# Softmax remainders and PSUM evictions moved between engines in a chain of three attention and feed-forward layers

## Chip, core and metric

The kernel runs on one core of a Trainium2 chip. The metric is the device time of one execution in microseconds (us); the median of three runs stands for a kernel.

## What is computed

Three layers in float32, each feeding the next, cut here to what matters:

```python
# 1: attention, B=4, H=8, S=1152, D=64; queries are pooled by two: T=576
q_pool = q.reshape(B, H, S // 2, 2, D).mean(axis=3)
a = softmax(q_pool @ k.T / sqrt(D));  x = a @ v            # x: (B, T, H*D = 512)
# 2: four causal attention heads over x, each token weighted by its two best gates
for e in range(4): out += gate[e] * (softmax(causal((x @ wq[e]) @ (x @ wk[e]).T / 8)) @ (x @ wv[e])) @ wo[e]
# 3: token shift, k = relu(xk @ w_k), r = sigmoid(xr @ w_r), result r * ((k * k) @ w_v)
```

## The kernel before

Layer 1 works head by head, 32 heads (four batches of eight). A head has nine **steps**; a step makes two score tiles of 128 keys by 288 queries in one PSUM buffer `st` (two such buffers), with two rounded (float32r) matmuls each (L760, L761: rounded keys and queries, then the products of their remainders and the row of the maxima). ScalarE takes the exponential into `p` (L768). The weighted sums over the keys follow four steps later (`LAG`), in one of two forms, which a table of nine entries per head chooses:

- **native** (`'n'`): one full-precision matmul a tile, `p` with the values `VF` (L788);
- **split**: `p` is copied into a rounded `ph` by the engine of the entry's first letter (L64 is ScalarE, `'s'`), the remainder `pl = p - ph` is taken by that of the second (L71; `'g'` is POOL, `'v'` is VectorE), and three rounded matmuls a tile follow: L795 and L796 (`ph` with rounded values and their remainders, in `VV`) and L797 (`pl`).

Ahead of a head the maxima of its scores are found: fifteen matmuls of 384 keys (L730), each reduced by VectorE from one of four PSUM banks (L732); L403 and L408 finish them. The weighted sums themselves occupy banks of the same four. When a sum is complete, `copy_eps` reads its bank into `U` (L142 on VectorE, L140 on ScalarE), and after a division (L254, and L256 with the gate) and a broadcast through DRAM (`R`), L817 writes the head's part of `XT`. `s2_split` turns a batch's `XT` into a rounded `XH` (L269) and a remainder `XL` (L270); `s1_vsplit` does so with the values of a head (L610, L611). `copy` is the helper behind L64 (ScalarE), L66 (VectorE) and L68 (POOL), `lo_of` that behind L71.

From batch 1 on, the steps of layer 2 for the batch before are set between the steps of layer 1 (`s2_job`: L470 to L476 scores, L482 exponentials, L498 sums, L531 the product with the gate). Weights of layer 3 are split into rounded parts in chunks `w3st` (L887 to L920). Layer 3 itself runs at the end (L1101, L1124, L1137).

The order of work comes from `drive`, which runs the steps one by one and lets each task (maxima, transposes, loads, splits) run its parts between two given steps, and from a scheduler that then places every instruction in its engine's queue.

The table that the change edits is `G` (L26); it is read where the work is built:

```python
how = G["SA" if hh == 0 else "SB" if hh == 1 else "S1" if b else "S0"][si]
copy(how[0], ph, pt)                                   # L774, in the step
lo_of(how[1], pl, pt, ph)                              # L780, two steps later
copy_eps(G["ua" if hh < 2 else "u1" if b else "u0"], U[...], acc[j][: D + 1, :HT])
copy_eps(G["u2"], U[...], acc[j][: D + 1, :HT])        # L523, layer 2
copy(G["vvh"] if hh > 2 else G["ve"], vt[:, :, 0:D], vr)
copy(G["xh"], XH[:, p], XT[:, p])
```

Of the kernel before, what the change touches and what calls it, by code (L numbers as in the profile page):

```python
# [22 lines left out]

P = 128
D = 64
G = {'LAG': 4, 'LO': 2, 'nf1': 2, 'nfx': 1, 'mxA': (0, 5), 'prA': (0.5, 5.0), 'mx0': (-2.0, 7.0), 'mx1': (-2.5, 6.0), 'vl': (0.0, 1.5), 'vs': (5.5, 1.0), 'pr0': (0.5, 5.0), 'pr1': (0.5, 4.0), 'ld': (6.5, 5.5), 'm2': (2.0, 1.5), 'nm': 0, 'nm2': 0, 'dup': 2, 'mid': 1, 'bc': 1, 'end': 9, 'mid2': 2, 'end2': 4, 'spl': 9, 'gate': 8, 'gate2': 2, 'w2': (2, 30), 'w3': (7, 14), 'S0': ('n', 'sv', 'sg', 'n', 'sv', 'n', 'sv', 'sv', 'sv'), 'S1': ('sg', 'sg', 'sv', 'sg', 'sg', 'sg', 'sv', 'n', 'sg'), 've': 'g', 'kh0': 's', 'kh1': 'v', 'qh0': 's', 'qh1': 's', 'kq': 's', 'kl': 'v', 'rs': 'v', 'rl': 'v', 'ym': 'g', 'yo': 'v', 'LGe': 'v', 'p1': (5, 5, 5, 9), 'p2': (9, 9, 9), 'p3': (2,), 'p4': (9, 9, 9, 9), 'p5': (8, 8, 8, 8), 'p6': (9, 9, 9), 'po': (2, 4, 5, 9), 'add0': 'g', 'add1': 'g', 'xt': 'v', 'u1': 'v', 'u2': 'v', 'y2': 'v', 'yh': 's', 'yl': 'v', 'xo': 'v', 'v2': 's', 'xh': 'g', 'xl': 'v', 'vvh': 'g', 'vvl': 'g', 'klo': 'v', 'HB': 3, 'PB': 6, 'blk': 1, 'm2w': 2, 'order': 2, 'kdup': 0, 'L2': 4, 'O2': 1, 'a0': (5.0, 5.0), 'a1': (2.0, 2.5), 'a2': (0.0, 1.0), 'a3': (2.0, 2.0), 'r0': 2, 'NV': 2, 'NF': 2, 'SA': ('n', 'vg', 'sg', 'n', 'sv', 'n', 'sv', 'sv', 'sv'), 'SB': ('n', 'sv', 'sv', 'n', 'vv', 'n', 'sv', 'sv', 'sv'), 'ua': 'v', 'u0': 'v', 'xt0': 'v', 'w3d': 8, 'w3q': (3, 27), 'WC': 1, 'kb': 1, 'kst': 1, 'qst': 0, 'CW': 512, 'wt': 'v', 'wl': 'v', 'wa': 'v', 'WB': 1, 'mxg': 2, 'hq': 's', 'hpos': (0, 1, 11, 20)}  # L26
NEG = -1.0e30

TINY = 1.17e-9
# [26 lines left out]
def tile_kernel(ctx: ExitStack, tc: tile.TileContext, q, k, v, w_gate, wq, wk, wv, wo,  # L56
                mu_k, mu_r, w_k, w_v, w_r, out):
    nc = tc.nc
    LAG, LO, HB = G["LAG"], G["LO"], G["HB"]
    eng = {"g": nc.gpsimd, "v": nc.vector, "s": nc.scalar}  # L60

    def copy(e, dst, src):
        if e == "s":
            nc.scalar.activation(dst, src, AF.Copy)  # L64
        elif e == "v":
            nc.vector.tensor_copy(dst, src)  # L66
        else:
            nc.gpsimd.tensor_scalar(dst, src, 1.0, 0.0, op0=ALU.mult, op1=ALU.add)  # L68

    def lo_of(e, dst, src, hi):  # L70
        eng[e].tensor_tensor(dst, src, hi.bitcast(F32), op=ALU.subtract)  # L71
# [88 lines left out]
    def later(n, fn):  # L160
        pending.append((now[0] + n, fn))
# [82 lines left out]
    def normaliser(U, gate, name):  # L244
# [8 lines left out]
        def mid():  # L253
# [3 lines left out]
            nc.sync.dma_start(scr.rearrange("o (p i) -> (o p) i", p=D), rd)  # L257
            later(G["bc"], bcast)

# [43 lines left out]
    def s2_gate(b):  # L303
# [3 lines left out]
        def f():  # L307
# [22 lines left out]
            def g():  # L330
# [973 lines left out]
```

## Time and profile before

| | before |
|---|---|
| median of 3 runs | 1107.34 us (1106.95 to 1110.87) |
| profiled execution | 1109.79 us |
| its span, first to last instruction | 1108.0 us |
| granted TensorE clock, mean | 0.987 |
| TensorE matmul busy | 1031.3 us, 93% |
| VectorE busy | 843.1 us, 76% |
| ScalarE busy | 550.4 us, 50% |
| POOL busy | 414.4 us, 37% |

Engines are named PE (TensorE matmul), PEld (its weight load), DVE (VectorE), ACT (ScalarE), POOL (GpSimd) and SP (SyncE, which issues the DMAs). An instruction's row names its line, engine, operation, what it writes and reads, and its shape. A busy share is an average over stages. A wait is put down to what ended it last by the profile. A full-precision matmul (L788) leaves two records, so a native step has four.

### The profile page before, as it was taken

The page shows a single profiled execution, that of the slowest core. Times are in us where ns is not written, and L with a number is a line of the kernel's source. Part 1 is how long each engine was busy: PE and PEld are TensorE (multiplying, and loading weights), DVE is VectorE, ACT ScalarE, POOL GpSimd, SP SyncE. Part 2 cuts the span into 40 slices and gives each one's busy share as a digit, 9 for nine tenths or more (in the row PEclk, how much of TensorE's full clock was granted, in tenths as well). Part 3 has the DMA queues.
Part 4 walks back from the last instruction along what each step waited for, and adds up shares of the span by engine and source line. Part 5 has one row for each costly group of instructions (what it writes and reads, how often), then busy time and mean ns, then how long its engine had stood idle before and what let it go on. Part 6 is the DMA issues. An engine that isn't in the chain of part 4 may idle for free.

```text
span 1108.0 us, 18910 instructions
## 1 busy us (share of the span) xinstructions
PE 1031.3 (93%) x6800; PEld 908.1 (82%) x6800; DVE 843.1 (76%) x1664; ACT 550.4 (50%) x922; POOL 414.4 (37%) x378
## 2 busy tenths in 40 slices
PE   5999998999999999999999999997997899999998
PEld 4788888888888887788888888886875788888887
DVE  5899998789999888989987877885777624444442
ACT  5567665556566555665555565563444312222222
POOL 7343327446345544543664445363002001111110
PEclk9899999999999999999999999999998999999999
DMA  4656544445544544554444333246354321111100
GB/s 113 144 153 141 131 118 118 106 120 142 143 116 103 149 126 124 132 141 124 109 129 113 87 92 87 71 130 199 113 163 137 114 81 39 40 39 39 39 20 20
DMA packets 129099, 119.29 MB, mean 108 GB/s; under 512 B 63751, under 2 KB 91358, under 8 KB 129006
## 3 DMA queue, kind: packets, MB, share of 16 engines
q1 hardware_dynamic: 129006, 118.08, 40.3%
q8 instruction: 54, 0.88, 0.3%
q14 instruction: 39, 0.32, 0.1%
HBM read 63.24 MB, written 20.07 MB: 75 GB/s over the span
## 4 chain that ended last, share of the span: by engine, by line
PE 62%; DVE 21%; DMA 8%; ACT 4%; issue 3%; SPq 1%; POOL 1%; DVEq 0%; ACTq 0%; POOLq 0%
PE stw L1137 9%; PE sth L1101 7%; PE bank L730 6%; PE st L760 5%; DVE PM L732 5%; PE st L761 4%; PE str L1124 4%; DMA R<-scr 4%; PE bank L797 3%; PE bank L795 3%; PE bank L796 3%; PE bank L788 3%; PE stq L354 3%; PE bank L498 3%; DVE pl L71 2%
## 5 line engine op out<-in xcount | busy, mean ns | idle before, releaser
L71 POOL TENSOR_TENSOR pl<-p,ph 128x576 fp32r<-128x576 f32 x152 | 230.6, 1521 | 208.9 <-ACT ph L64 115.7
L732 DVE TENSOR_REDUCE PM<-bank 128x1 f32<-128x384 f32 (+1 forms) x480 | 251.6, 543 | 30.3 <-PE bank L730 27.7
L768 ACT ACTIVATE p<-st 128x576 f32<-128x576 f32 x288 | 186.0, 648 | 117.0 <-PE st L761 111.9
L64 ACT ACTIVATE ph<-p 128x576 fp32r<-128x576 f32 x238 | 162.8, 685 | 57.8 <-PE bank L796 48.7
L730 PE MATMUL bank<-KA,QA 128*128 128x384 f32 (+1 forms) x480 | 177.8, 383 | 13.7 <-DVE KB L151 4.4
L760 PE MATMUL st<-QA,KA 128*128 128x288 f32 x576 | 177.5, 319 | 3.9 <-DVE LG L299 1.7
L761 PE MATMUL st<-QB,KB 65*128 65x288 f32 x576 | 167.5, 305 | 0.0
L797 PE MATMUL bank<-pl,VV 128*65 128x288 f32 x480 | 142.4, 297 | 8.4 <-DVE pl L71 6.1
L795 PE MATMUL bank<-ph,VV 128*65 128x288 f32 x480 | 145.0, 302 | 2.0 <-DVE PM L732 0.8
L796 PE MATMUL bank<-ph,VV 128*64 128x288 f32 x480 | 141.6, 295 | 0.0
L760 PEld LDWEIGHTS st<-QA,KA 128*128 128x128 f32 x576 | 110.9, 193 | 12.5 <-ACT p L768 4.0
L761 PEld LDWEIGHTS st<-QB,KB 65*128 65x128 f32 x576 | 110.7, 193 | 2.5 <-issue 0.2
L730 PEld LDWEIGHTS bank<-KA,QA 128*128 128x128 f32 (+1 forms) x480 | 87.1, 185 | 28.8 <-DVE PM L732 9.5
L1040 POOL TENSOR_SCALAR yxr<-x,omr 128x256 f32<-128x256 f32 x36 | 25.7, 730 | 196.3 <-DVE xkl L151 133.4
L1101 PE MATMUL sth<-xkh,wk 128*128 128x256 f32 x512 | 91.3, 279 | 1.2 <-ACT relu L1108 1.2
L71 DVE TENSOR_TENSOR pl<-p,ph 128x576 fp32r<-128x576 f32 x88 | 79.4, 903 | 1.8 <-ACT ph L64 1.1
L1101 PEld LDWEIGHTS sth<-xkh,wk 128*128 128x128 f32 x512 | 78.7, 188 | 1.9 <-ACT relu L1108 1.4
L1108 ACT ACTIVATE relu<-sth 128x512 f32<-128x512 f32 x32 | 17.5, 597 | 121.1 <-PE sth L1101 120.3
L797 PEld LDWEIGHTS bank<-pl,VV 128*65 128x65 f32 x480 | 65.3, 136 | 11.2 <-DVE pl L71 7.2
L795 PEld LDWEIGHTS bank<-ph,VV 128*65 128x65 f32 x480 | 66.1, 138 | 6.6 <-DVE PM L732 2.3
L1101 PE MATMUL sth<-xkl,wk 128*128 128x256 f32 x256 | 71.4, 279 | 0.0
L796 PEld LDWEIGHTS bank<-ph,VV 128*64 128x64 f32 x480 | 65.3, 136 | 6.3 <-issue 0.2
(209 smaller groups left out, 2326.0 us busy)
## 6 DMA issues: line engine op xcount, KB each, us to landing
KA<-sk SPq DMA_DIRECT2D x60, 160.0 KB
qr<-in_q_dram SPq DMA_DIRECT2D x32, 288.0 KB
kr<-in_k_dram SPq DMA_DIRECT2D x32, 288.0 KB
VF<-in_v_dram SPq DMA_DIRECT2D x32, 288.0 KB
KA<-sk SPq DMA_DIRECT2D x60, 128.0 KB
R<-scr SPq DMA_DIRECT2D x48, 144.0 KB
w3h<-w3st SPq DMA_DIRECT2D x20, 256.0 KB
w3l<-w3st SPq DMA_DIRECT2D x20, 256.0 KB
```

Source lines behind the costliest of these rows:

```text
L64: nc.scalar.activation(dst, src, AF.Copy)
L71: eng[e].tensor_tensor(dst, src, hi.bitcast(F32), op=ALU.subtract)
L730: nc.tensor.matmul(ps[:n, : 3 * P], QA[i][:, t0 : t0 + n], KA[i][:, 3 * g * P : 3 * (g + 1) * P], start=True, stop=True)
L732: nc.vector.tensor_reduce(pm[:n, c, g : g + 1], ps[:n, : 3 * P], axis=AX.X, op=ALU.max)
L760: nc.tensor.matmul(st[:, n, :HT], KA[i][:, ks], QA[i][:, cs], start=True, stop=False)
L761: nc.tensor.matmul(st[:, n, :HT], KB[i][0 : D + 1, ks], QB[i][0 : D + 1, cs], start=False, stop=True)
L768: nc.scalar.activation(pt, st[:, :, :HT], AF.Exp, scale=1.0 / 16.0)
L795: nc.tensor.matmul(a[: D + 1, :HT], vh, ph[:, n], start=c == 0, stop=False)
L796: nc.tensor.matmul(a[:D, :HT], vl, ph[:, n], start=False, stop=False)
L797: nc.tensor.matmul(a[: D + 1, :HT], vh, pl[:, n], start=False, stop=c == NC - 1)
L1101: nc.tensor.matmul(st[:, f // 2, f % 2 * GT : (f % 2 + 1) * GT], w[kt][:, fs], x[:, kt], start=i == 0, stop=i == 3 * KT - 1)
L1137: nc.tensor.matmul(st[:, c], x[:, f, ts], w[f], start=i == 0, stop=i == 3 * FT - 1)
```

## The change

One line changes, the table `G`. The entries that differ, one to a line:

```diff
-'S0': ('n', 'sv', 'sg', 'n', 'sv', 'n', 'sv', 'sv', 'sv')
-'S1': ('sg', 'sg', 'sv', 'sg', 'sg', 'sg', 'sv', 'n', 'sg')
+'S0': ('n', 'sv', 'sv', 'n', 'sv', 'sv', 'n', 'sv', 'sv')
+'S1': ('n', 'sv', 'sv', 'n', 'sv', 'sv', 'n', 'sv', 'sv')
...
-'u0': 'v', 'u1': 'v', 'u2': 'v'
+'u0': 's', 'u1': 's', 'u2': 's'
...
-'vvh': 'g', 'xh': 'g'
+'vvh': 's', 'xh': 's'
```

`S0` holds for heads 2 to 7, `S1` for heads 8 to 31. In `S1` native steps go from one to three, remainders on POOL from six to none, remainders on VectorE from two to six. In `S0` one remainder moves from POOL to VectorE and one native step moves from place 5 to place 6. Evictions of the sums (`u0`, `u1`, `u2`) go from VectorE to ScalarE in all heads but the first two and in layer 2; the rounding copies of the values from head 3 on and of `XT` go from POOL to ScalarE. Maxima are taken in pieces of 384 keys in both kernels.

**VectorE where head 19 ends and head 20 begins.** `pl_19_6` is the remainder of head 19, step 6; `PM` are the pieces of the maxima, `nm` their end. Before:

```order
L732 TENSOR_REDUCE PM_196<-bank_6142 64x1
L732 TENSOR_REDUCE PM_197<-bank_6166 128x1
L403 TENSOR_REDUCE nm_20_6160<-PM_196 128x5
L817 TENSOR_TENSOR XT<-U_18_5852,R_18_5958 64x2x3x96
L409 CAST mr_20_6176<-bank_6175 5x128
L732 TENSOR_REDUCE PM_197<-bank_6193 128x1
L71 TENSOR_TENSOR pl_19_6_6154<-p_19_6_6151,ph_19_6_6153 128x576
L732 TENSOR_REDUCE PM_197<-bank_6210 128x1
L142 TENSOR_SCALAR U_19_6216<-bank_6083,epsc 65x288
L732 TENSOR_REDUCE PM_197<-bank_6233 128x1
L732 TENSOR_REDUCE PM_197<-bank_6247 128x1
```

The changed kernel:

```order
L71 TENSOR_TENSOR pl_19_4_5920<-p_19_4_5917,ph_19_4_5919 128x576
L403 TENSOR_REDUCE nm_20_5969<-PM_196 128x5
L732 TENSOR_REDUCE PM_197<-bank_5975 128x1
L71 TENSOR_TENSOR pl_19_5_5949<-p_19_5_5946,ph_19_5_5948 128x576
L409 CAST mr_20_5985<-bank_5984 5x128
L732 TENSOR_REDUCE PM_197<-bank_6003 128x1
L817 TENSOR_TENSOR XT<-U_18_5675,R_18_5779 64x2x3x96
L732 TENSOR_REDUCE PM_197<-bank_6017 128x1
L71 TENSOR_TENSOR pl_19_7_5997<-p_19_7_5994,ph_19_7_5996 128x576
L732 TENSOR_REDUCE PM_197<-bank_6038 128x1
L531 TENSOR_TENSOR U_1_0_5802<-U_1_0_5802,R_1_0_5878 64x576
```

A remainder now stands after every one or two reductions, where before there was one in this stretch, and the eviction `U_19` is no longer in the queue.

**ScalarE in head 20.** `p_20_2` is the exponential of step 2, `VV` the rounded values of head 21. Before:

```order
L64 ACTIVATE ph_20_1_6259<-p_20_1_6257 128x576
L768 ACTIVATE p_20_2_6284<-st_20_2_6279 128x576
L768 ACTIVATE p_20_3_6313<-st_20_3_6308 128x576
L64 ACTIVATE ph_20_2_6286<-p_20_2_6284 128x576
L64 ACTIVATE QA_188<-bank_6319 64x288 x2
L768 ACTIVATE p_20_4_6353<-st_20_4_6348 128x576
```

The changed kernel:

```order
L768 ACTIVATE p_20_2_6085<-st_20_2_6080 128x576
L64 ACTIVATE ph_20_2_6087<-p_20_2_6085 128x576
L768 ACTIVATE p_20_3_6117<-st_20_3_6112 128x576
L64 ACTIVATE QA_188<-bank_6120 64x288 x2
L140 ACTIVATE U_19_6023<-bank_6025,epsc 65x288
L64 ACTIVATE VV_191<-VF_193 128x9x64
L768 ACTIVATE p_20_4_6154<-st_20_4_6149 128x576
L64 ACTIVATE ph_20_4_6156<-p_20_4_6154 128x576
```

Between the exponentials of steps 3 and 4 ScalarE now evicts head 19's sum and copies the values of the next head; step 3 is native and has lost its copy `ph`.

## Rows read from the trace of the kernel before

**Rows 1.** The page, part 1: busy time, share of the span, instructions.

```profile
PE 1031.3 (93%) x6800; PEld 908.1 (82%) x6800; DVE 843.1 (76%) x1664; ACT 550.4 (50%) x922; POOL 414.4 (37%) x378
```

**Rows 2.** Busy time by stretch; columns: stretch, length, PE, PEld, DVE, ACT, POOL, clock, DMA.

```profile
95.00:161.00 66.00, 65.03 (x438) 58.45 (x436) 62.75 (x130) 44.45 (x74) 19.57 (x18) 1.00 0.57 133
161.00:357.00 196.00, 184.54 (x1279) 163.50 (x1277) 176.88 (x359) 116.05 (x195) 101.70 (x76) 0.99 0.48 120
357.00:561.00 204.00, 190.54 (x1327) 168.66 (x1325) 187.76 (x372) 118.17 (x199) 102.27 (x76) 1.00 0.50 128
561.00:761.00 200.00, 187.81 (x1314) 168.02 (x1315) 154.14 (x316) 111.20 (x185) 100.38 (x81) 0.99 0.42 107
876.00:1108.00 232.00, 226.36 (x1321) 198.70 (x1321) 100.98 (x154) 57.34 (x84) 33.54 (x52) 0.99 0.12 40
```

**Rows 3.** Chain of waits, 357 to 561 us: share by line; its longest piece of stq.

```profile
by line: DVE PM L732 10.2%; PE bank L730 6.1%; issue 5.8%; DMA R<-scr 5.2%; PE st L760 4.9%; PE st L761 4.8%; PE bank L797 3.5%; DVE pl L71 3.5%; PE bank L796 3.5%; PE bank L498 3.4%; PE bank L795 3.4%; PE sto L550 3.2%; PE stq L354 3.1%; D
...
408.89 3.19 PE stq L354 x24
```

**Rows 4.** Chain of waits, 95 to 161 us: one native step.

```profile
96.02 0.97 PE bank L788 x4
```

**Rows 5.** Line 71 alone, 357 to 561 us: DVE busy (count), POOL busy (count).

```profile
357.00:561.00 204.00, 29.29 (x30) 84.72 (x56) 1.00 0.50 128
```

**Rows 6.** DVE groups, 357 to 561 us: count | busy, mean ns | idle.

```profile
L142 DVE TENSOR_SCALAR U<-bank,epsc 65x288 f32<-65x288 f32 x24 | 12.1, 505 | 2.3 <-PE bank L797 1.9 <-PE bank L498 0.2
L817 DVE TENSOR_TENSOR XT<-U,R 64x576 f32<-64x576 f32 x8 | 9.4, 1176 | 2.2 <-DMA R<-scr 2.1
L888 DVE TENSOR_SCALAR w3st<-w3st 128x512 int32<-128x512 int32 x6 | 5.6, 925 | 0.0
L898 DVE SCALAR_TENSOR_TENSOR w3st<-w3st 128x512 f32<-128x512 f32 x6 | 5.2, 861 | 0.4
L904 DVE TENSOR_SCALAR w3st<-w3st 128x512 int32<-128x512 int32 x6 | 3.7, 616 | 0.1
L256 DVE TENSOR_TENSOR rd<-rd,GR 64x9 f32<-64x9 f32 x4 | 3.1, 777 | 0.0
```

**Rows 7.** The remainders on DVE, 95 to 161 us.

```profile
L71 DVE TENSOR_TENSOR pl<-p,ph 128x576 fp32r<-128x576 f32 x20 | 14.9, 746 | 0.3 <-ACT ph L64 0.2
```

**Rows 8.** DVE by line and form, 800 to 876 us, where POOL does little.

```profile
L898 DVE SCALAR_TENSOR_TENSOR w3st<-w3st 128x512 f32<-128x512 f32 x5 | 3.4, 686 | 0.1
L531 DVE TENSOR_TENSOR U<-U,R 64x576 f32<-64x576 f32 x4 | 3.0, 749 | 3.5 <-DMA R<-scr 3.4
L904 DVE TENSOR_SCALAR w3st<-w3st 128x512 int32<-128x512 int32 x6 | 2.5, 419 | 0.1
L888 DVE TENSOR_SCALAR w3st<-w3st 128x512 int32<-128x512 int32 x5 | 2.1, 428 | 10.6 <-DMA w3st<-in_moe_w_v_dram 10.6
L256 DVE TENSOR_TENSOR rd<-rd,GR 64x9 f32<-64x9 f32 x4 | 0.8, 206 | 0.1
```

**Rows 9.** POOL by line and form, 357 to 561 us: what stays there.

```profile
L71 POOL TENSOR_TENSOR VV<-VF,VV 128x576 fp32r<-128x576 f32 x8 | 10.9, 1358 | 0.6
L627 POOL TENSOR_TENSOR qp<-qr 96x384 f32<-96x384 f32 x8 | 8.5, 1058 | 15.3 <-PE bank L683 15.3
```

**Rows 10.** ACT by line and form, 357 to 561 us: a read of PSUM.

```profile
L64 ACT ACTIVATE QA<-bank 64x288 fp32r<-64x288 f32 x16 | 6.5, 404 | 2.2 <-PE bank L683 1.9
```

**Rows 11.** Waits of PE, 561 to 761 us: total, times, longest.

```profile
PE bank L797 <- DVE pl L71: 3.9, 2, 3.2
```

**Rows 12.** Waits of PE, 161 to 357 us.

```profile
PE bank L797 <- POOL pl L71: 2.0, 1, 2.0
```

**Rows 13.** Timeline of ACT, 416 to 422.5 us: start, length, what.

```profile
417.49 0.65 ACT L768 ACTIVATE p<-st 128x576 f32<-128x576 f32 x1 [0.75 <-PE st L761]
420.25 0.65 ACT L768 ACTIVATE p<-st 128x576 f32<-128x576 f32 x1 [1.02 <-PE st L761]
```

**Rows 14.** Timeline of POOL, the same stretch.

```profile
421.17 0.67 POOL L68 TENSOR_SCALAR VV<-VF 128x576 fp32r<-128x576 f32 x1 [2.92 <-PE bank L427]
```

More of the change, by code (lines that the diff above doesn't have):

```diff
@@ L25 @@
 D = 64
-G = {'LAG': 4, 'LO': 2, 'nf1': 2, 'nfx': 1, 'mxA': (0, 5), 'prA': (0.5, 5.0), 'mx0': (-2.0, 7.0), 'mx1': (-2.5, 6.0), 'vl': (0.0, 1.5), 'vs': (5.5, 1.0), 'pr0': (0.5, 5.0), 'pr1': (0.5, 4.0), 'ld': (6.5, 5.5), 'm2': (2.0, 1.5), 'nm': 0, 'nm2': 0, 'dup': 2, 'mid': 1, 'bc': 1, 'end': 9, 'mid2': 2, 'end2': 4, 'spl': 9, 'gate': 8, 'gate2': 2, 'w2': (2, 30), 'w3': (7, 14), 'S0': ('n', 'sv', 'sg', 'n', 'sv', 'n', 'sv', 'sv', 'sv'), 'S1': ('sg', 'sg', 'sv', 'sg', 'sg', 'sg', 'sv', 'n', 'sg'), 've': 'g', 'kh0': 's', 'kh1': 'v', 'qh0': 's', 'qh1': 's', 'kq': 's', 'kl': 'v', 'rs': 'v', 'rl': 'v', 'ym': 'g', 'yo': 'v', 'LGe': 'v', 'p1': (5, 5, 5, 9), 'p2': (9, 9, 9), 'p3': (2,), 'p4': (9, 9, 9, 9), 'p5': (8, 8, 8, 8), 'p6': (9, 9, 9), 'po': (2, 4, 5, 9), 'add0': 'g', 'add1': 'g', 'xt': 'v', 'u1': 'v', 'u2': 'v', 'y2': 'v', 'yh': 's', 'yl': 'v', 'xo': 'v', 'v2': 's', 'xh': 'g', 'xl': 'v', 'vvh': 'g', 'vvl': 'g', 'klo': 'v', 'HB': 3, 'PB': 6, 'blk': 1, 'm2w': 2, 'order': 2, 'kdup': 0, 'L2': 4, 'O2': 1, 'a0': (5.0, 5.0), 'a1': (2.0, 2.5), 'a2': (0.0, 1.0), 'a3': (2.0, 2.0), 'r0': 2, 'NV': 2, 'NF': 2, 'SA': ('n', 'vg', 'sg', 'n', 'sv', 'n', 'sv', 'sv', 'sv'), 'SB': ('n', 'sv', 'sv', 'n', 'vv', 'n', 'sv', 'sv', 'sv'), 'ua': 'v', 'u0': 'v', 'xt0': 'v', 'w3d': 8, 'w3q': (3, 27), 'WC': 1, 'kb': 1, 'kst': 1, 'qst': 0, 'CW': 512, 'wt': 'v', 'wl': 'v', 'wa': 'v', 'WB': 1, 'mxg': 2, 'hq': 's', 'hpos': (0, 1, 11, 20)}
@@ new lines @@
+G = {'LAG': 4, 'LO': 2, 'nf1': 2, 'nfx': 1, 'mxA': (0, 5), 'prA': (0.5, 5.0), 'mx0': (-2.0, 7.0), 'mx1': (-2.5, 6.0), 'vl': (0.0, 1.5), 'vs': (5.5, 1.0), 'pr0': (0.5, 5.0), 'pr1': (0.5, 4.0), 'ld': (6.5, 5.5), 'm2': (2.0, 1.5), 'nm': 0, 'nm2': 0, 'dup': 2, 'mid': 1, 'bc': 1, 'end': 9, 'mid2': 2, 'end2': 4, 'spl': 9, 'gate': 8, 'gate2': 2, 'w2': (2, 30), 'w3': (7, 14), 'S0': ('n', 'sv', 'sv', 'n', 'sv', 'sv', 'n', 'sv', 'sv'), 'S1': ('n', 'sv', 'sv', 'n', 'sv', 'sv', 'n', 'sv', 'sv'), 've': 'g', 'kh0': 's', 'kh1': 'v', 'qh0': 's', 'qh1': 's', 'kq': 's', 'kl': 'v', 'rs': 'v', 'rl': 'v', 'ym': 'g', 'yo': 'v', 'LGe': 'v', 'p1': (5, 5, 5, 9), 'p2': (9, 9, 9), 'p3': (2,), 'p4': (9, 9, 9, 9), 'p5': (8, 8, 8, 8), 'p6': (9, 9, 9), 'po': (2, 4, 5, 9), 'add0': 'g', 'add1': 'g', 'xt': 'v', 'u1': 's', 'u2': 's', 'y2': 'v', 'yh': 's', 'yl': 'v', 'xo': 'v', 'v2': 's', 'xh': 's', 'xl': 'v', 'vvh': 's', 'vvl': 'g', 'klo': 'v', 'HB': 3, 'PB': 6, 'blk': 1, 'm2w': 2, 'order': 2, 'kdup': 0, 'L2': 4, 'O2': 1, 'a0': (5.0, 5.0), 'a1': (2.0, 2.5), 'a2': (0.0, 1.0), 'a3': (2.0, 2.0), 'r0': 2, 'NV': 2, 'NF': 2, 'SA': ('n', 'vg', 'sg', 'n', 'sv', 'n', 'sv', 'sv', 'sv'), 'SB': ('n', 'sv', 'sv', 'n', 'vv', 'n', 'sv', 'sv', 'sv'), 'ua': 'v', 'u0': 's', 'xt0': 'v', 'w3d': 8, 'w3q': (3, 27), 'WC': 1, 'kb': 1, 'kst': 1, 'qst': 0, 'CW': 512, 'wt': 'v', 'wl': 'v', 'wa': 'v', 'WB': 1, 'mxg': 2, 'hq': 's', 'hpos': (0, 1, 11, 20)}
```

## The prediction

> **What bounds the kernel now.** I read the page first, then busy time by stretch, the chain of waits, the groups by line and form, and last the timeline of one place. Engine shares over the whole span [rows 1] name TensorE at 93% and VectorE at 76%, but that average mixes three regimes, and the stretches separate them [rows 2]. From 95 to 161 us (heads of batch 0) TensorE is busy 65.0 of 66 us: it binds, and nothing that shortens another engine shows. From 161 to 561 us (batches 1 and 2) VectorE is busy 176.9 of 196 and 187.8 of 204 us, 90 and 92%, and the chain of waits goes through the reductions of the maxima on VectorE more than through any other line [rows 3]: here VectorE paces the kernel and TensorE waits for banks and operands. From 561 to 761 us (batch 3) VectorE falls to 154 of 200 us and TensorE holds 187.8. From 876 us to the end TensorE is busy 226 of 232 us on a part that the change doesn't touch. So two stretches are to be costed on VectorE, one on TensorE.
>
> **The change, part by part.** I take 357 to 561 us (eight heads of batch 2, four jobs of the second attention) and use it for batch 1 too, whose loads are alike [rows 2].
>
> *Native steps.* In batches 1 to 3 each head goes from one native step to three: 48 steps swap six 288-column matmuls for two in full precision. A native step takes 0.97 us on the chain, four records [rows 4]; 24 matmuls of 288 columns take 3.19 us, so six take 0.80 [rows 3]. TensorE gets 0.17 us a step, 2.8 us a batch, 8.3 in all. Between 161 and 561 us TensorE is the engine that waits, so I charge nothing there; were that cover gone it would be 5.6 us. In batch 3 I charge half, 1.4 us, between nothing and 2.8. ScalarE loses 48 rounding copies, TensorE nothing else. In batch 0 the number of native steps stays three; only the place of one moves, which I cost at nothing.
>
> *Remainders.* Per head six `pl` subtractions stand on VectorE instead of two: 32 more in the stretch. Line 71 on VectorE is now 30 operations in 29.29 us, 0.98 each [rows 5]; beside a POOL that works 20 of 66 us the same subtraction takes 0.746 [rows 2, 7]. After the change there are 62. At 0.746 they take 46.3 us: **plus 17.0**. POOL's own subtractions (84.7 less the 10.9 of `VV`, 73.8 us) and its copies go; of 102.3 us the `VV` remainders and the `qp` additions stay, 19.4 us or 19% [rows 2, 5, 9]. If the excess of 0.23 us per operation falls in that proportion, 62 operations keep 0.19 times 0.23 each: **plus 2.7**.
>
> *Other operations beside POOL.* `XT` takes 1176 ns where a product of the same shape takes 749 with POOL nearly idle; L888 925 against 428, L898 861 against 686, L904 616 against 419, L256 777 against 206 [rows 6, 8]. By their counts that is 3.4, 3.0, 1.1, 1.2 and 2.3, together 11.0 us of delay in this stretch. Of it 81% goes: **minus 8.9**; bounds are nothing and 11.0.
>
> *Evictions.* 24 reads of the weighted sums leave VectorE, 12.1 us, and with them 2.3 us in which VectorE stood idle until TensorE had finished a sum [rows 6]: **minus 12.1 and minus 2.3**. On ScalarE a read of 64x288 from PSUM takes 404 ns [rows 10]; 24 of them are 9.7 us. With the copies of V and XH that come from POOL (12 at about the 0.65 of a 576-wide activation [rows 13], 7.8 us), and without 16 copies of `ph` (10.4), ScalarE gains 7 us on 118 of 204 [rows 2]: time it has.
>
> VectorE in this stretch: 17.0 + 2.7 - 8.9 - 12.1 - 2.3 = **-3.6 us**, and as VectorE paces it, the stretch shortens by that. What is late next is TensorE, at 190.5 of 204. Heads 2 to 7 of batch 0 are bound by TensorE with equal work: nothing, as the two evictions that leave a head and the one remainder that comes both lie beside it. Behind 761 us eight evictions move: nothing.
>
> Sum: twice -3.6, plus 1.4, is **-5.8 us**. The profiled execution took 1109.8 us, so 1104.0; the median of the runs shown is 2.4 lower, so **1101.5**. About 0.5% (5.5 us) is what a measurement of this kernel can tell from no change, and the forecast lies at that edge.
>
> One rule bears on the 19%. The rows show only the averages above. The Trainium skill (SBUF — State Buffer, Who interferes with whom) says that a VectorE instruction with two SBUF inputs and a GpSimd instruction that reads SBUF exclude each other for the whole instruction, whoever comes second waiting. By that rule it is not the share of POOL's time that counts but how often the two meet. The trace so far agrees in direction, 0.98 against 0.746 us, and doesn't tell the two ways apart; what it would give is the first rival.
>
> **Rivals.** *(a) The delay doesn't fall with POOL's time.* VectorE will have twice as many two-input operations, so each of the 16 POOL operations that stay in a stretch may still hold one up. If each costs half its length, 8 times 0.68 and 8 times 0.53 [rows 9], 9.7 us remain instead of 2.7 plus 2.1: VectorE's -3.6 becomes +1.3. With 1.4 in batch 3, the sum is +4.0 at most; with half of that effect, -1: **1107 to 1111**, no change. For it: `XT` at 1176 shows that a single meeting costs much. Against: the 0.746 beside a POOL 30% busy.
>
> *(b) Slower: remainders queue behind maxima.* VectorE takes its work in order, and the third matmul of a sum (L797) can't start without its `pl`. In batch 3, 17 remainders on VectorE already cost TensorE 3.9 us in two waits, the longest 3.2 [rows 11]. With 48 at that rate it is 11.0, 7.1 more; if the two earlier stretches lose their 3.6 us in the same way, the result is 1101.5 + 7.1 + 7.2, **1116**. It decides once a `pl` stands more than the four steps between an exponential and its sum behind in VectorE's queue. For it: the order now puts a remainder after nearly every pair of reductions. Against: POOL's own remainder is longer and made L797 wait as well, 2.0 us from 161 to 357 us [rows 12], and that wait goes.
>
> *(c) Slower: exponentials wait behind copies.* The copy of V now stands on ScalarE between two exponentials. At 421.17 us POOL began one that had waited for TensorE; the exponential ahead of its place in the new order ended at 418.14, the next began at 420.25 [rows 13, 14]. In order, that next one would start at 421.84, 1.6 us late. In 24 heads that is 38 us of delay, of which the two score tiles in PSUM hide most; a third of it reaching TensorE gives **1114**. The Trainium skill (PSUM — Partial Sum Buffer, Engine vs sequencer instructions) calls ScalarE's queue strictly first in, first out; that is the condition of this rival, and nothing here contradicts it.
>
> That the change does not do what it says can be left out: the order of the new kernel shows the six remainders, the evictions and the copies on the engines named.
>
> **How the numbers follow.** Forecast 0.45, rival (a) 0.27, (b) 0.16, (c) 0.12. The forecast's own range: with all of the delay gone twice 4.8 us more (1092), with the native steps paid in full 1.4 plus 5.6 more (1108). The range that holds 8 in 10 takes in (a), all but the lowest tail of the forecast, and (b): 1090 to 1117. Faster by over 0.5%: most of the forecast's half that lies below 1101.8, and what of it goes further since waits on banks fall too, 0.42. Within 0.5%: the rest of the forecast and (a) but for its slow end, 0.34. Slower: (b), most of (c), a little of the forecast, 0.24.
>
> **What would show it.** VectorE: 190 `pl` near 0.76 us, `XT` near 0.8, L888 near 0.45, no L142 beyond the first heads, busy time from 357 to 561 us a few us lower. POOL busy near 20 us in that stretch. ScalarE: evictions near 0.4 us, no long idle time ended by DMA or TensorE ahead of copies of V. TensorE: 192 more records on L788, its idle time ended by VectorE smaller. I am wrong on the size of the contention if `pl` stays above 0.85; on the pace if VectorE's busy time falls and the stretch doesn't; and rival (b) holds if L797's waits for `pl` pass 10 us.

## The result and the profile after

The changed kernel takes **1082.79 us** (median of five runs, 1081.44 to 1089.10), the kernel before beside it 1109.24. The ratio is 0.977, with a 95% interval of 0.9743 to 0.9796: faster by 2.3%. The direction was the forecast's, the size was not: 26.5 us against 5.8, and the range began at 1090.

The profiled execution is the longest of the five, 1089.1 us with a span of 1087.4. The run `e10_write_decoy` below, whose queues on TensorE and ScalarE are the same instruction by instruction, is 4.7 us shorter in head 22 (24.5 us instead of 29.2) and 1.8 in head 23. In head 22 of this execution a broadcast of `R` took 6.04 us on the chain; a product on VectorE waited for it, the remainder behind that product came late, and TensorE idled for 2.36 us at L797. From 524.5 to 534.8 us its clock was then granted at 1.2 GHz, half of 2.4 (columns: stretch, length, PE, clock, DMA):

```profile
524.50:534.80 10.30, 10.30 (x46) 0.50 0.01 2
```

Where the size of a stretch matters, both runs are given.

The page's part 1, after, to be set beside [rows 1]:

```profile
PE 1038.8 (96%) x6704; PEld 902.5 (83%) x6704; DVE 818.5 (75%) x1674; ACT 578.3 (53%) x1011; POOL 160.0 (15%) x183
```

Busy time by stretch, after; columns as in [rows 2]. The stretches begin where the same heads begin (head 8 at 159, head 16 at 349, head 24 at 549 us):

```profile
95.00:159.00 64.00, 63.42 (x425) 56.83 (x423) 60.84 (x125) 48.62 (x86) 11.34 (x8) 1.00 0.53 130
159.00:349.00 190.00, 185.11 (x1246) 158.87 (x1246) 165.96 (x357) 120.93 (x215) 20.55 (x17) 1.00 0.49 120
349.00:549.00 200.00, 195.51 (x1296) 169.97 (x1295) 173.70 (x372) 122.73 (x218) 19.98 (x16) 0.97 0.50 126
549.00:739.00 190.00, 187.25 (x1277) 163.36 (x1276) 158.02 (x335) 117.69 (x207) 21.57 (x20) 1.00 0.45 117
```

From 159 us on POOL falls to a fifth, TensorE rises to 97% and more, VectorE goes from 90 and 92% to 87%. Taking each head from its first score matmul (L760), the time came from here:

| us | before | after | `e10_write_decoy` |
|---|---|---|---|
| heads 2 to 7 | 99.8 | 98.3 | 98.4 |
| heads 8 to 15 (batch 1) | 196.1 | 189.8 | 189.9 |
| heads 16 to 23 (batch 2) | 203.7 | 199.9 | 193.6 |
| heads 24 to 30 | 176.3 | 173.5 | 173.7 |
| head 31 | 23.7 | 17.2 | 17.5 |
| layer 2's rest and layer 3 | 347.4 | 348.0 | 348.9 |

VectorE's groups of the stretch 349 to 549 us, after, by form; they answer to [rows 6] and [rows 7], and the first row has 48 remainders of 0.751 us:

```profile
L71 DVE TENSOR_TENSOR pl<-p,ph 128x576 fp32r<-128x576 f32 x48 | 36.0, 751 | 1.2 <-ACT ph L64 0.9
L817 DVE TENSOR_TENSOR XT<-U,R 64x576 f32<-64x576 f32 x8 | 6.0, 747 | 1.4 <-DMA R<-scr 1.3
L898 DVE SCALAR_TENSOR_TENSOR w3st<-w3st 128x512 f32<-128x512 f32 x5 | 3.4, 684 | 0.1
L904 DVE TENSOR_SCALAR w3st<-w3st 128x512 int32<-128x512 int32 x5 | 2.1, 424 | 0.1
L888 DVE TENSOR_SCALAR w3st<-w3st 128x512 int32<-128x512 int32 x5 | 2.1, 420 | 2.3 <-DMA KA<-sk 1.9 <-DMA w3st<-in_moe_w_r_dram 0.2
L256 DVE TENSOR_TENSOR rd<-rd,GR 64x9 f32<-64x9 f32 x4 | 0.6, 153 | 0.0
```

Every operation that was longer beside POOL is at its undisturbed length. The evictions on ScalarE, the same stretch, took 0.49 us each, not the 0.40 of the smaller read in [rows 10]:

```profile
L140 ACT ACTIVATE U<-bank,epsc 65x288 f32<-65x288 f32 x25 | 12.3, 492 | 7.1 <-DVE XT L817 2.1 <-PE bank L797 2.1 <-PE bank L498 1.6
```

TensorE's waits from 160 to 740 us, before (us in total, times, longest), the five largest:

```profile
PE bank L424 <- DVE PM L732: 6.5, 5, 1.9
PE bank L408 <- DVE nm L403: 4.7, 7, 0.9
PE sto L550 <- ACT YH L64: 2.6, 2, 1.3
PE bank L797 <- DVE pl L71: 2.2, 2, 1.1
PE bank L797 <- POOL pl L71: 2.0, 1, 2.0
```

and after:

```profile
PE bank L797 <- DVE pl L71: 3.2, 3, 2.4
PE bank L408 <- DVE nm L403: 3.0, 6, 1.0
PE bank L730 <- DVE PM L732: 1.4, 2, 0.7
```

Added over all rows of that view that end in VectorE, TensorE waited 24.5 us for VectorE before and 8.5 after (5.7 in `e10_write_decoy`). That sum is used for every run below and called **TensorE's waits for VectorE**. Its window is the same for all runs, so it leaves out the end of the heads in the slower ones: up to 761 us, the kernel before has 28.4. For `pl` made on POOL TensorE waited 2.3 us in all of these heads before, so remainders that come late from POOL are a small part of what the change removed, at most.

Head 31 gave 6.5 us where the forecast had nothing. Here [rows 11] has its 3.9 us on L797. The long wait of the two, before (VectorE, then TensorE):

```profile
755.23 0.75 DVE L817 TENSOR_TENSOR XT<-U,R 64x576 f32<-64x576 f32 x1 [3.27 <-DMA R<-scr]
756.71 0.35 PE L797 MATMUL bank<-pl,VV 128*65 128x288 f32 x1 [3.24 <-DVE pl L71]
```

Between the two VectorE made the `pl` that L797 needs, at 755.91 us: it stood in the queue behind `XT`, which waited for the broadcast of `R`. From 757.3 to 760.7 us TensorE then ran at 1.2 GHz. After, from 722 to 740 us, one wait of 0.3 us on `pl` is left. The division ahead of that broadcast (L254) began 12.0 us into the head before and 7.2 after. The chain leads to it through a remainder of 1.98 us on VectorE and through the first mixes of layer 3, which stood between remainders on POOL; that POOL made it late is argued from this and not tested by itself.

### The profile page after: what moved, and what is told of

The parts are those of the page before. It is cut to its first block, busy times and chain, and to the rows that moved or that the text cites. A ratio compares the mean times of both kernels' runs of the same rounds, so it can differ in the third digit from the quotient of the medians.

```text
span 1087.4 us, 18428 instructions
## 1 busy us (share of the span) xinstructions
PE 1038.8 (96%) x6704; PEld 902.5 (83%) x6704; DVE 818.5 (75%) x1674; ACT 578.3 (53%) x1011; POOL 160.0 (15%) x183
## 4 chain that ended last, share of the span: by engine, by line
PE 70%; DVE 10%; DMA 10%; ACT 6%; issue 2%; POOL 1%; SPq 1%; DVEq 0%; ACTq 0%; POOLq 0%
PE stw L1137 9%; PE sth L1101 8%; PE bank L730 6%; PE bank L788 6%; PE st L760 5%; PE st L761 5%; PE str L1124 4%; PE bank L797 3%; PE bank L796 3%; PE bank L795 3%; PE stq L354 3%; DMA R<-scr 3%; PE bank L498 2%; DVE PM L732 2%; PE stv L287 2%
## 5 line engine op out<-in xcount | busy, mean ns | idle before, releaser
L760 PE MATMUL st<-QA,KA 128*128 128x288 f32 x576 | 178.5, 321 | 1.5 <-ACT p L768 0.5
L71 DVE TENSOR_TENSOR pl<-p,ph 128x576 fp32r<-128x576 f32 x190 | 143.6, 758 | 4.2 <-ACT ph L64 3.2
L64 ACT ACTIVATE ph<-p 128x576 fp32r<-128x576 f32 x190 | 129.7, 684 | 15.2 <-PE bank L796 5.8
L760 PEld LDWEIGHTS st<-QA,KA 128*128 128x128 f32 x576 | 111.0, 193 | 13.6 <-ACT p L768 4.9
L788 PE MATMUL bank<-p,VF 128*65 128x288 f32 x384 | 118.3, 406 | 0.5 <-DVE QA L151 0.2
L795 PE MATMUL bank<-ph,VV 128*65 128x288 f32 x384 | 117.0, 305 | 0.0
L797 PE MATMUL bank<-pl,VV 128*65 128x288 f32 x384 | 113.9, 297 | 3.2 <-DVE pl L71 3.2
L796 PE MATMUL bank<-ph,VV 128*64 128x288 f32 x384 | 113.6, 296 | 0.0
L71 POOL TENSOR_TENSOR VV<-VF,VV 128x576 fp32r<-128x576 f32 x32 | 42.6, 1332 | 305.7 <-ACT VV L64 253.1
L627 POOL TENSOR_TENSOR qp<-qr 96x384 f32<-96x384 f32 x31 | 39.4, 1269 | 250.0 <-PE bank L683 155.8
L788 PEld LDWEIGHTS bank<-p,VF 128*65 128x65 f32 x384 | 50.8, 137 | 15.5 <-ACT U L140 1.0
L1109 DVE TENSOR_TENSOR relu<-relu 128x512 f32<-128x512 f32 x32 | 20.8, 688 | 55.0 <-ACT relu L1108 55.0
```

Source lines behind the costliest of these rows:

```text
L760: nc.tensor.matmul(st[:, n, :HT], KA[i][:, ks], QA[i][:, cs], start=True, stop=False)
L788: nc.tensor.matmul(a[: D + 1, :HT], VF[hh % NF][:, c], cell["p"][:, n], start=c == 0, stop=c == NC - 1)
L795: nc.tensor.matmul(a[: D + 1, :HT], vh, ph[:, n], start=c == 0, stop=False)
L796: nc.tensor.matmul(a[:D, :HT], vl, ph[:, n], start=False, stop=False)
L797: nc.tensor.matmul(a[: D + 1, :HT], vh, pl[:, n], start=False, stop=c == NC - 1)
```

## The experiments

All ratios are to the kernel before, measured beside each run on the same chip, with their 95% intervals; "busy" is VectorE's on the page.

| run | ratio | median us | VectorE busy | TensorE's waits for VectorE |
|---|---|---|---|---|
| before | 1 | | 843.1 | 24.5 |
| changed kernel | 0.977 [0.9743, 0.9796] | 1082.8 | 818.5 | 8.5 |
| e1_tables | 0.9909 [0.9881, 0.9937] | 1101.6 | 868.2 | 9.2 |
| e2_evict | 1.0109 [1.0056, 1.0162] | 1126.0 | 810.9 | 33.7 |
| e3_copies | 0.9988 [0.9962, 1.0013] | 1110.4 | 837.6 | 25.1 |
| e5_tables_evict | 0.9834 [0.979, 0.9878] | 1093.9 | 827.3 | 5.9 |
| e11_tables_copies | 0.9838 [0.9813, 0.9863] | 1091.3 | 855.7 | 5.4 |
| e7_decoy | 1.0062 [1.0035, 1.0089] | 1118.2 | 861.7 | 18.9 |
| e12_read_decoy | 0.9954 [0.9931, 0.9978] | 1104.0 | 841.4 | 14.1 |
| e10_write_decoy | 0.9792 [0.9738, 0.9845] | 1087.8 | 818.7 | 5.7 |
| e19_vector_work | 0.9887 [0.9833, 0.994] | 1098.2 | 853.6 | 4.6 |
| e4_one_native | 0.981 [0.9758, 0.9862] | 1090.1 | 852.3 | 8.5 |
| e13_rest_on_vector | 0.9828 [0.9802, 0.9854] | 1091.0 | 846.0 | 8.7 |
| e6_three_native_pool | 1.0068 [1.0046, 1.009] | 1118.8 | 770.5 | 26.0 |
| e9_four_native | 0.9912 [0.9878, 0.9946] | 1100.2 | 808.0 | 7.0 |

### The parts of the change

```diff
 # e1_tables: before, with
+'S0': ('n', 'sv', 'sv', 'n', 'sv', 'sv', 'n', 'sv', 'sv')    and the same for 'S1'
 # e2_evict: before, with
+'u0': 's', 'u1': 's', 'u2': 's'
 # e3_copies: before, with
+'vvh': 's', 'xh': 's'
 # e5_tables_evict: e1 and e2 together     # e11_tables_copies: e1 and e3 together
```

> The kernel before with the new tables S0 and S1 alone; evictions stay on VectorE, rounding copies of the values and of XT on POOL. Three theories. Load of VectorE (its two-input operations slowed by POOL, and its evictions): with 10.8 us more on VectorE in each of the two stretches that it paces, 1125 to 1132 us. Evictions (the gain of the change is theirs): no gain here, 1105 to 1130. Late remainders (a remainder on POOL comes late because POOL is slow and works in order; taking it off POOL is the gain): 1085 to 1095, most of the gain.

> The kernel before with the evictions (u0, u1, u2) alone on ScalarE. Load of VectorE: 14.4 us less on VectorE in each of two stretches, of which TensorE lets perhaps two thirds through, 1088 to 1095. Evictions: the whole gain, 1080 to 1087. Late remainders: POOL is as before, 1103 to 1109.

> The kernel before with the rounding copies of the values and of XT alone on ScalarE. Load of VectorE: POOL loses 9 of 102 us in a stretch, VectorE about 1 us, 1106 to 1109. Evictions: no change, 1107 to 1111. Late remainders: POOL's queue is 12 operations shorter in a stretch, 1102 to 1107.

> Tables and evictions of the change, the rounding copies of the values and of XT still on POOL. Collision theory: POOL keeps 9 us of a stretch that read one operand, 1083 to 1090. Late remainders: 1083 to 1090. If the copies matter on ScalarE (its queue), this is faster than the change, 1075 to 1081.

> The changed kernel with its evictions of the weighted sums back on VectorE (as before), all else as changed. Theory (collisions make VectorE late; once they are gone the evictions are plain work that VectorE sheds): what the evictions gave on top of the new steps alone, 0.9909 to 0.9834 of the kernel before, is lost again, about 1091 us. Rival (the evictions cost something by themselves, as they did alone, 1.0109): this kernel is faster than the changed one, about 1071 us.

The tables alone bring 0.9%, though VectorE's busy time rises by 25 us. The copies alone bring nothing that can be told. The evictions alone make the kernel **slower by 1.1%**, though VectorE's busy time falls by 32 us. On top of the tables the same evictions bring 0.75% (0.9909 to 0.9834), and on top of tables and copies 0.7% (0.9838 to 0.977); the copies bring 0.6 to 0.7% on top of the tables, with the evictions or without. So the parts don't add: 0.9 gained, 1.1 lost and nothing make 2.3 gained together. The theory's 1091 us for e11 was met; its rival, that evictions have one sign wherever they stand, fell. Of the earlier expectations, e1, e2 and e5 lie outside every range given for them; for e3, no change was one of the three.

What evictions alone do is seen in TensorE's waits, 160 to 740 us, of e2:

```profile
PE bank L408 <- DVE nm L403: 11.1, 16, 1.1
PE bank L730 <- DVE PM L732: 5.8, 4, 2.2
PE bank L424 <- DVE PM L429: 4.3, 2, 2.3
```

and in TensorE's busy time and granted clock in heads 8 to 15 and 16 to 23 (stretch, length, busy, clock, DMA), first before, then e2:

```profile
160.80:356.90 196.10, 184.64 (x1280) 0.99 0.48 120
356.90:560.60 203.70, 190.35 (x1327) 1.00 0.50 128
```

```profile
160.80:366.40 205.60, 188.21 (x1278) 0.98 0.47 116
366.40:582.70 216.30, 195.86 (x1328) 0.96 0.47 119
```

These 16 heads take 22.1 us longer in e2, and the rest of the kernel 5.5 less. TensorE is idle there for 13.0 us more, and busy for 9.1 more with the same matmuls: the clock was granted at 1.2 instead of 2.4 GHz seven times, for 27 us in all, against 3 before. So more than half of the loss there is waiting, and the rest goes with the lower clock. Each of the seven falls came some microseconds behind an idle time of 1.4 to 2.3 us on TensorE; that the idle time brought it about is argued from this order.

### Collisions, or POOL's time

Three runs add work to POOL in the changed kernel whose result nobody reads. In all three the queues of TensorE, ScalarE, SyncE and VectorE are those of the changed kernel, instruction by instruction (in e10 two rows of VectorE's are swapped). POOL must be done with `p` before ScalarE can write that buffer again: ScalarE's exponentials waited for POOL 8.4 us in e7, 8.5 in e10, 10.0 in e12 and not at all in the changed kernel, so the three runs hardly differ in that. The place is behind each of the 144 remainders of batches 1 to 3:

```diff
 lo_of(how[1], pl, pt, ph)
+if b: decoy(pt)          # junk: a tile that nobody reads
 # e7:  gpsimd.tensor_tensor(junk, pt, pt, subtract)
 # e12: twice gpsimd.tensor_scalar(junk, pt, 1.0, 0.0, mult, add)
 # e10: gpsimd.tensor_copy of one element of pt, then twice gpsimd.memset(junk, 0.0)
```

> The changed kernel, and beside each of the six remainders of heads 8 to 31 POOL subtracts p from itself into a tile that nothing reads (144 operations of the shape of the remainders that POOL had before; extra work, the result is as before). The queues of TensorE, VectorE, ScalarE and SyncE are the same instruction by instruction. Collision theory (POOL's subtractions stretch VectorE's two-input operations, and that is what the change removes): most of the gain is lost, 1098 to 1110 us, pl back near 1.0 us. Late-remainder theory (POOL's remainders came late): nothing waits for POOL here, 1083 to 1088. Order theory (the gain is that the new queue order fits the chip better): the order is the same, 1083 to 1088.

> As the kernel with the subtractions, but POOL reads one element of p and then writes zeros to the tile twice (144 times; extra work, the result is as before): POOL about as busy, with next to no reading of SBUF. Collision theory: VectorE's two-input operations stay at 0.75 us, 1083 to 1090. Late remainders and order: 1083 to 1088. If it is as slow as the other, it is POOL's time and not what it reads.

> The changed kernel with 144 pairs of POOL copies of p into a tile that nobody reads (each copy one SBUF input, a pair about as long as one of the 144 subtractions that cost 35 us); every other queue is the same instruction by instruction. If any POOL read of SBUF holds up VectorE's two-input operations: pl near 0.88 again and about 1115 us. If it takes two inputs on POOL: pl stays near 0.76, and the time within 6 us of the changed kernel, 1080 to 1089.

POOL's groups in e7, in e10 and in e12, and behind each VectorE's remainders:

```profile
L157 POOL TENSOR_TENSOR junk<-p 128x576 f32<-128x576 f32 x144 | 187.8, 1304 | 247.1 <-ACT p L768 244.8
L71 DVE TENSOR_TENSOR pl<-p,ph 128x576 fp32r<-128x576 f32 x190 | 172.0, 908 | 3.4 <-ACT ph L64 2.5
```

```profile
L157 POOL MEMSET junk<- 128x576 f32 x288 | 167.8, 583 | 16.9 <-POOL junk L157 0.2
L71 DVE TENSOR_TENSOR pl<-p,ph 128x576 fp32r<-128x576 f32 x190 | 143.7, 759 | 3.9 <-ACT ph L64 3.1
```

```profile
L157 POOL TENSOR_SCALAR junk<-p 128x576 f32<-128x576 f32 x288 | 253.2, 879 | 194.6 <-ACT p L768 178.3
L71 DVE TENSOR_TENSOR pl<-p,ph 128x576 fp32r<-128x576 f32 x190 | 155.8, 822 | 3.5 <-ACT ph L64 2.6
```

144 subtractions that nobody reads take back all of the gain and more: 35 us of span against e10, 30 us by the medians (the profiled execution of e10 was the fastest of its four). They are dearer than any of the three theories said. As the order of the queues is the same, the gain isn't due to the order alone. POOL is as busy in e10 (373 us) as in e7 (348), and e10 costs nothing that can be told; so it is not POOL's time or its queue. In e12 POOL reads as many bytes with one input an instruction, and the remainder is held up by 0.06 us instead of 0.15; the expectations of e12, "as e7" and "nothing", were both missed, as it stands between, 17 us of span against e10. Two-input and one-input reads both hold VectorE up.

The Trainium skill (SBUF — State Buffer, Who interferes with whom) says that a VectorE instruction with two SBUF inputs contends with a GpSimd instruction that reads SBUF and not with one that only writes it. The three runs agree with both halves, 908 and 822 ns against 759.

The price: from e10 to e7 VectorE's busy time rises by 43.0 us and the span by 34.8 (1082.5 to 1117.3); from e10 to e12 by 22.7 and 17.2. **A microsecond of delay on VectorE cost 0.8 of span, 0.7 to 0.8 by the medians.** Some of it is the lower clock: TensorE ran at 1.2 GHz for 14 us of the heads in e7, never in e10. TensorE's waits, 160 to 740 us, of e7:

```profile
PE bank L408 <- DVE nm L403: 7.3, 10, 1.8
PE stq L354 <- ACT p L768: 4.5, 2, 4.3
PE bank L730 <- DVE PM L732: 4.5, 4, 1.4
PE sto L550 <- ACT YH L64: 3.5, 2, 2.0
```

The waits are spread over the places where a late VectorE meets TensorE's fixed order, and two stand at ScalarE; that a late VectorE had held ScalarE up in turn is likely and not shown.

### VectorE's work, without collisions

```diff
 # e19_vector_work: the changed kernel, at the same 144 places
+if b: vector.memset(junk[:, 0, 0:256], 0.0)
 # e4_one_native: the changed kernel, with
+'S1': ('sv', 'sv', 'sv', 'sv', 'n', 'sv', 'sv', 'sv', 'sv')
 # e13_rest_on_vector: the changed kernel, with
+'vvl': 'v', 'add0': 'v', 'add1': 'v'
```

> The changed kernel with 144 writes of 128x256 zeros on VectorE into a tile that nobody reads, one ahead of each place where e7 had its POOL subtraction: some 0.3 us each, 43 us in all, as long as e7's delay on VectorE. The order of the queues is made with them in it. If work is as dear as delay (0.8 us per us): 1115 us. If work that the order holds finds room beside TensorE (0.1 to 0.3 us per us, as the runs with more remainders suggest): 1087 to 1096 us.

> The changed kernel with one native step a head instead of three in heads 8 to 31, all eight remainders on VectorE: TensorE 8.3 us less in all, VectorE 48 remainders or 36 us more, ScalarE 48 copies more. If VectorE paces heads 9 to 24 still: 1092 to 1105. If TensorE paces now: 1075 to 1083. Order theory: no forecast.

> The changed kernel with the last two-input operations of POOL in the heads (the VV remainders, the qp additions) moved to VectorE too, some 32 of 0.75 us and 31 of about 0.5 us. Theory (what is left of the collisions is small: pl 0.758 against 0.746): VectorE only gains work, 40 us over 31 heads in places where it has room in part, 1083 to 1095 us. Rival (the few collisions that are left still cost several us each, as those of the subtractions did): 1070 to 1078 us.

e19 adds 39.2 us of work to VectorE in batches 1 to 3. Busy time by stretch (columns as in [rows 2]), heads 8 to 15, 16 to 23 and 24 to 30, in e19:

```profile
168.20:354.70 186.50, 183.71 (x1246) 159.24 (x1245) 173.14 (x391) 120.31 (x213) 21.12 (x17) 1.00 0.49 121
354.70:548.40 193.70, 190.26 (x1294) 165.87 (x1294) 178.84 (x405) 123.15 (x217) 20.07 (x16) 1.00 0.52 129
548.40:726.80 178.40, 173.18 (x1175) 151.71 (x1174) 160.87 (x362) 106.02 (x188) 16.62 (x13) 0.99 0.43 106
```

and in e7, the same heads:

```profile
160.50:356.50 196.00, 187.46 (x1244) 160.29 (x1244) 173.38 (x355) 120.76 (x214) 83.65 (x64) 0.99 0.47 116
356.50:560.50 204.00, 193.04 (x1296) 165.79 (x1295) 188.14 (x372) 122.72 (x217) 81.32 (x64) 1.00 0.49 124
560.50:750.70 190.20, 176.22 (x1173) 153.15 (x1173) 163.88 (x319) 106.02 (x187) 71.58 (x57) 0.97 0.40 98
```

In e19 these 23 heads take 558.6 us with VectorE busy for 512.9 (92%), in e7 590.2 with 525.4 (89%), in e10 557.2. Work of nearly the same length as e7's delay costs 1.4 us there instead of 33. In all, e19 is still 1.2% slower than the changed kernel and 2 us outside of what was expected. Its span is 13.4 us longer than e10's, 0.34 us for a microsecond of work, mostly for a reason elsewhere: its order differs from the first head on, and before head 2 it loses 8 us, 7.1 of them in one wait of TensorE's:

```profile
PE st L760 <- DVE QA L151: 7.1, 1, 7.1
```

e4 and e13 point the same way with useful work: 34 and 28 us more on VectorE cost 0.4 and 0.6% in the whole (e4 also spares TensorE 48 native steps, 8 us by the forecast's 0.17 each, and lies between its two expectations). In e13 hardly any POOL operation with two inputs is left in the heads, and that brings no further gain; what remains of collisions after the change is small.

That the order makes room for work which it knows, and can't for a delay which it doesn't, is the reading that fits. It isn't shown by itself, as e19's work came together with a new order.

### Less work on VectorE, and slower

```diff
 # e6_three_native_pool: the changed kernel, with
+'S1': ('n', 'sg', 'sg', 'n', 'sg', 'sg', 'n', 'sg', 'sg')
 # e9_four_native: the changed kernel, with
+'S1': ('n', 'sv', 'n', 'sv', 'n', 'sv', 'n', 'sv', 'sv')
 # later: one step more ahead of the transpose of the maxima (L408)
+'nm': 1      # e15: in the changed kernel, e16: in e2, e17: in e6, e18: in e9
```

> The changed kernel, but in heads 8 to 31 the six remainders of each head are on POOL; three native steps, evictions and copies stay as in the change. Load of VectorE: VectorE sheds its remainders in these heads, but every two-input operation there is slowed by POOL again, about as much as in the kernel before; VectorE is far from full, so 1080 to 1090. Evictions: as the change, 1080 to 1086. Late remainders: POOL has its 144 remainders back, 1098 to 1108.

> The changed kernel with four native steps instead of three in batches 1 to 3: TensorE gets 24 times 0.17 us, 4 us; VectorE loses 24 remainders of 0.76 us, 18 us. If TensorE binds now (96% busy): 1087 us. If VectorE's lateness still sets part of the time: 1072 to 1080 us.

e6 is the changed kernel with the six remainders of each head on POOL. VectorE's busy time is the lowest of all, 770.5 us, and the kernel is slower than before, outside all three expectations. TensorE's largest waits, 160 to 740 us:

```profile
PE bank L408 <- DVE nm L403: 17.9, 18, 3.3
PE bank L730 <- DVE PM L732: 4.0, 5, 1.3
PE bank L730 <- ACT U L140: 2.4, 1, 2.4
```

In the order, the matmuls between the last piece of a head's maxima and the transpose that needs their end have some 5100 columns before and 5000 after, but 4200 in e6, 4400 in e9 and 4500 in e2 (mean of heads 9 to 31, counted in the traces, a full-precision column twice). With a lighter VectorE the order had put the transposes nearer. Four runs emitted them a step later, which makes it 7200 columns and more:

> The kernel before with evictions on ScalarE (1.0109 alone) and the transposes of the maxima one step later in TensorE's order. Place theory (the lighter VectorE let TensorE's queue take the transpose too early, and VectorE, late by collisions, made it wait 12.5 us at L408): that wait falls under 3 us and the time to 1100 to 1110 us, a ratio of 0.99 to 1.00. Rival (the copies on ScalarE themselves hold TensorE up): 1120 us or more.

> The kernel with three native steps and six remainders on POOL (1.0068) and the transposes one step later. Place theory: L408's wait of 18 us goes, and 10 us or more with it, 1095 to 1108 us. Rival: 1115 us or more, as the row of maxima now comes later to the scores.

> The changed kernel with the transposes one step later. Its L408 waits are 3.0 us in all, so the place theory gives 1078 to 1083 us; the rival, a row of maxima that arrives too late for the scores, 1090 us or more.

> The kernel with four native steps (1100.2 us) and the transposes one step later. L408's waits there are only 1.3 us, its waits for ScalarE 7.9 us, so by the place theory this gives little, 1095 to 1100 us; if the close place were behind all of its loss against three native steps, 1080 to 1085 us.

| run | without | a step later |
|---|---|---|
| e16, on e2 | 1.0109 [1.0056, 1.0162] | 1.0064 [1.0042, 1.0087] |
| e17, on e6 | 1.0068 [1.0046, 1.009] | 0.9978 [0.996, 0.9995] |
| e15, on the changed kernel | 0.977 [0.9743, 0.9796] | 0.9868 [0.9842, 0.9894] |
| e18, on e9 | 0.9912 [0.9878, 0.9946] | 0.9909 [0.9882, 0.9936] |

The waits at L408 went as expected, in e16 from 11.1 to 3.9 us and in e17 from 17.9 to 5.2, but the time followed only in e17 (0.9%, just short of the expected range) and hardly in e16, which lies between its two expectations. TensorE's waits in e16:

```profile
PE bank L730 <- DVE PM L732: 4.8, 3, 2.2
PE st L761 <- DMA QB<-mr: 4.7, 6, 1.2
PE bank L424 <- DVE PM L732: 4.1, 4, 1.4
PE bank L795 <- DVE PM L732: 3.9, 5, 1.7
```

A late VectorE is met at the next place instead, and the row of maxima now comes late to the scores. In the changed kernel the later transpose costs 1%, as the rival had it. The place of L408 is thus a part of what e6 lost and not the cause in e2. Why four native steps are slower than three (1.4%, missing both expectations) stays open: its waits for VectorE are small, and those for ScalarE are 7.9 us against 1.5 (4.0 in e10).

## Why the prediction was wrong in size

**What bounds: half right.** VectorE does make TensorE late from 161 to 561 us, and its waits fell from 24.5 to 8.5 us. But the prediction read 90 and 92% busy as a pace. The chain that it read with that [rows 3] has 13.7% in VectorE's two lines shown and some 36% in TensorE's. e19 holds VectorE at 92% in 23 heads at a loss of 1.4 us, and e2 and e6 lower its busy time and lose. Busy time was the wrong measure; in these runs it is how late particular instructions come that TensorE waits for.

**The step that failed** is "VectorE in this stretch: 17.0 + 2.7 - 8.9 - 12.1 - 2.3 = -3.6 us, and as VectorE paces it, the stretch shortens by that". Its terms, measured in the stretch after:

- *Remainders, plus 17.0 and 2.7.* All of L71 on VectorE went from 29.29 us [rows 5] to 45.81 for 62 operations: plus 16.5. The residual contention of 2.7 was not there.

```profile
349.00:549.00 200.00, 45.81 (x62) 10.65 (x8) 0.97 0.50 126
```

- *Other operations beside POOL, minus 8.9.* The five groups counted gave, at their undisturbed means for the same counts, 3.4 + 3.0 + 1.1 + 1.2 + 2.5 = 11.2 us, the whole of the 11.0 and not 81% of it. Smaller groups that weren't counted gave another 4.4: six L893 0.8, four L436 1.4, one L320 1.2, four L531 0.7, L917 0.3. Together minus 15.6. Operations with one input (L888, L904, L320) lost as well as those with two. Two of the small groups before, and below the same after:

```profile
L436 DVE TENSOR_TENSOR PM<-PM 64x1 f32<-64x1 f32 x4 | 1.9, 486 | 0.0
L320 DVE TENSOR_SCALAR g_ct<-g_ct 128x20 f32<-128x20 f32 x1 | 1.4, 1354 | 0.0
```

```profile
L436 DVE TENSOR_TENSOR PM<-PM 64x1 f32<-64x1 f32 x4 | 0.6, 141 | 0.0
L320 DVE TENSOR_SCALAR g_ct<-g_ct 128x20 f32<-128x20 f32 x1 | 0.2, 178 | 0.0
```

- *Evictions, minus 12.1 and 2.3*: as forecast.

With the right sizes the same sum is 16.5 - 15.6 - 12.1 - 2.3 = -13.5, not -3.6. The delay was thus undersized by 9.9 us in this stretch, 6.7 here and 3.2 in the remainders. The second half of the step, that the stretch shortens by as much, is wrong too: VectorE's busy time fell by 10.9 and 14.1 us in batches 1 and 2, and they shortened by 6.3 and 10.1 (203.7 to 193.6, in e10; 3.8 in the profiled execution of the change), about two thirds of it. Over the whole kernel: 102 more subtractions at 0.758 are 77.3 us, 92 evictions less at 0.505 are 46.5; VectorE would have gained 30.8 us of work and fell by 24.6 (843.1 to 818.5), so **55 us of delay went**. The prediction removed some 26: in each of two stretches 17.9 (30 times 0.23 and 11.0) less the 4.8 that were to stay.

The sum also set work against delay at par. The runs price them apart: 0.7 to 0.8 for a microsecond of delay; for one of work that the order holds next to nothing in those 23 heads, and 0.34 over the whole kernel in e19. Why the change itself returned 26.5 us for 55 of delay was not tested; one bound is seen in batch 2, where TensorE was busy for 190.3 of 203.7 us before and is for 191.4 of 193.6 in e10, so there was little more to be had.

**The proportion of POOL's time failed as a rule.** The 19% stood for how much delay would be left. Its rival was that the number of meetings counts. After the change almost nothing is left (0.751 us for a remainder, 0.747 for `XT`) although 16 POOL operations remain in the stretch, so rival (a) fell as well; and e10 shows POOL's time to be no measure, as 215 us of its writes and one-element reads delay nothing.

**Places costed at nothing.** Head 31 gave 6.5 us: a remainder stood behind a product that waited for a DMA, and the lower clock followed. Behind the heads the forecast's nothing held (347.4 and 348.0), heads 2 to 7 gave 1.5, and heads 24 to 30 gave 2.8 where 1.4 of loss had been charged, though TensorE took the longer native steps.

**Rivals (b) and (c)** fell. L797's waits for `pl` are 3.2 us from 160 to 740 us, under the 10 that was set as the mark. TensorE's waits for ScalarE were 3.0 us before and 1.5 after (4.0 in e10), far from the third of 38 us. The 0.492 us of an eviction on ScalarE was 22% above the estimate, and harmless.

**The marks** set for the profile were met on VectorE (`pl` 0.758, `XT` 0.748, L888 0.428 over the kernel), on POOL (20.0 us) and on TensorE; VectorE's busy time fell by 14 us in the stretch, not by "a few".

## What to carry to other kernels

Before costing a move between VectorE and POOL, list every VectorE operation that reads SBUF and runs longer than its like in a quiet stretch, the small ones too, and count that whole excess as delay which goes with POOL's reads; in these runs delay weighed more than twice as much as work that the order knew. Don't read a busy share of 90% as the bound: look at how long the bound engine's consumers wait for it, and test with work that nobody reads. Look also for what stands in an engine's queue behind an operation that waits for a DMA: twice here a remainder did, and TensorE idled for 2.4 and 3.2 us. And a part of a change that hurts by itself may help once the rest is in, so try parts in both contexts.

## What the runs showed that was not expected

- POOL writing 144 pairs of 128x576 tiles (0.58 us each) costs VectorE nothing; 144 reads of the same tile with two inputs cost 35 us of span of 1083 (30 by the medians), and 144 pairs of reads with one input 17.
- Small operations suffer most in proportion: a 64x1 product took 486 ns beside POOL and 141 without, a 128x20 one 1354 and 178.
- VectorE at 92% over 559 us, in a fixed order beside a TensorE at 98%, cost 1.4 us of time there.
- Taking 46.5 us of evictions off VectorE made the kernel before slower by 1.1%, and TensorE's mean granted clock there fell to 0.98 and 0.96 in the two batches that had 0.99 and 1.00.
